# Written-out orders of work on every engine, and narrower warm-up matmuls in a PSUM bank of their own, in a four-layer linear-attention and SwiGLU kernel

## The chip, the core and the metric

The kernel runs on one core of a Trainium2 chip. The metric is the device time of one execution in microseconds, as the median of five runs. The engines have short names here: PE is TensorE (PEld its weight loads, which overlap its matmuls), DVE is VectorE, ACT is ScalarE, POOL is GpSimd, and SP is SyncE, which only issues DMAs.

## The reference

Two kinds of layer alternate, A, B, A, B (layers 0 to 3 below), on 2048 tokens of width 512; the weights of both A layers are the same, and so are those of both B layers. Everything is bf16.

```
x = A_x
x = x + A(layernorm(x), wqkv, wo)        # layer 0
x = x + B(layernorm(x), gate, up, down)  # layer 1
x = x + A(layernorm(x), wqkv, wo)        # layer 2
x = x + B(layernorm(x), gate, up, down)  # layer 3

A: q, k, v = x @ wqkv, in 32 heads of 16
   phi(t) = where(t > 0, t + 1, exp(t)) + 1e-6
   kv = sum_s phi(k)^T v ;  z = sum_s phi(k)
   o  = phi(q) kv / (phi(q) z + 1e-6) ;  A = o @ wo
B: silu(x @ gate) * (x @ up) @ down      # inner width 1792
```

## The kernel before

The tokens are cut into 16 tiles of 128, and four tiles make a group. All weights and the residual `X` stay in SBUF. PSUM has eight banks of 128x512 f32, `PB[0]` to `PB[7]`. The work of PE is written as a list of tokens, `PROGRAM`, and the recording functions below turn each token into operations on all engines. A token names the layer, the kind of step and the tile or group:

- `S` is a spin: a matmul of zeros that keeps PE busy at the start and that nobody reads.
- `0t1` transposes the normalized tile 1 of layer 0 on PE, and ACT or DVE copies it out. Only tiles named in `PE_T` go this way. All others are transposed by a DMA that SP issues (`xT`).
- `0k4` is the key projection of tile 4, four matmuls of 512 columns. Behind it ACT takes `exp`; DVE clips it (`ts`) and takes the maximum with `1 + k` (`phi`). For tiles named in `ON_ACT` ACT also makes `1 + k` (`id1`), so that DVE's `phi` does not read PSUM.
- `0g4` adds tile 4 to the matrix x^T phi(k), in four banks that are held from the first to the last tile of the layer. `0z4` adds it to the sum of phi(k), in one more held bank.
- `0q12` is the query projection of group 1, part 2, with the same `phi`; `0d12` its denominator. `den` on DVE ends in a reciprocal. In most groups ACT then repeats 1/den (`rep`), a DMA transposes it (`rT`) and DVE multiplies (`pqn`). In groups of `PE_T` (`0d2`, `2d1`) the tokens `0r20` to `0r23` do the same on PE.
- `0v` and `0m0` to `0m3` fold the value and output weights into the matrix; each `m` is copied out of PSUM (`evac`).
- `0w3` is the attention output of tile 3. `res` on DVE adds it to `X`.
- `1u012` is one gate/up pair of a B layer for group 0, inner block 12: eight matmuls into two banks. ACT takes `tanh`, DVE does `gst` (times gate) and `h` (times up). `1n3` is the down projection of tile 3, fourteen matmuls, and its `res`.

Behind each `w` and `n` the next layernorm is recorded by `ln`: ACT takes the sum of squares (`sq`), POOL a scaled sum (`negm`), POOL or DVE `vpe`, POOL the power -1/2 (`pow`), and then DVE applies mean and scale (`apply`), or, for tiles named `0x5` and the like in `ON_ACT`, POOL makes one more product (`nmr`) and ACT applies it. In layer 0 the statistics of `X` come from DVE, or from ACT for tiles named `0s4` and the like. Below, `1x6.apply` is that step of the layernorm that feeds tile 6 of layer 1.

Buffers bind the steps. Layernorms of layers 1 and 3 go through three buffers `xnB` in turn, and ACT's `sq` writes its unused output there, so the `sq` of a tile waits until the DMA transpose of the tile three earlier has landed. The gate/up pairs share three buffers `tht` between `tanh` and `h`. A step that needs a bank takes the free one that was used longest ago.

`Prog.op` records an operation with its buffers read and written, its assumed duration and a kind. `Prog.schedule` keeps PE in the order of `PROGRAM` and chooses the order of every other engine while the program is built: it simulates the engines, and among the operations that could start within `HOLD` it takes the one with the earliest due time, shifted by a `BIAS` of its kind. `Prog.sync` then reduces the dependences to semaphore waits, and `emit` writes each engine's list. On the chip every engine works through its list strictly in order.

The large weights come by POOL's queue. `Wo`, the four pieces `Wg0` to `Wg3` and the four pieces of `Wu` are loaded behind the last DMA transpose of layer 0, `Wd` in four pieces behind the first four transposes of layer 1.

## Time and profile before

| | |
|---|---|
| median of 5 runs | 432.77 us (432.57 to 433.63) |
| profiled execution, its own time | 431.64 us |
| its span (first to last instruction) | 429.9 us |
| granted clock of PE in the span | 1.0 |
| busy: PE, DVE, ACT, POOL | 419.4, 290.5, 214.8, 79.9 us |
| one matmul of 512 columns in a stream | 379 ns from start to end, the next starts about 216 ns after it |

A matmul's row shows its whole way through the array; in a stream the next one starts long before it ends. So PE's idle time in the rows is the time without any matmul under way, and a gap in the stream is longer than that by about 0.16 us (379 less 216 ns).

### The profile page before, as it was taken

To read this page: it belongs to the slowest core of one execution; us is meant where nothing else is said; L and a number is where in the kernel's file an instruction comes from. 1 tells how busy PE (TensorE), PEld (TensorE's weight loads), DVE (VectorE), ACT (ScalarE), POOL (GpSimd) and SP (SyncE) were. 2 spreads that over 40 slices of the span, in tenths; PEclk is the share of its full clock that TensorE was granted. 3 is DMA by queue.
4 is the path that set the end of the run, shared out by engine and by line. 5 is a ranking of instruction groups with operands and counts; after the bars stand their busy time and mean duration, and the time that the engine had idled before them with its cause. 6 is when DMAs were issued, how large, how long until landed. Compare 5 with 4: busy or idle time off the path is not lost.

```text
span 429.9 us, 6498 instructions
## 1 busy us (share of the span) xinstructions
PE 419.4 (98%) x2188; PEld 194.9 (45%) x2231; DVE 290.5 (68%) x593; ACT 214.8 (50%) x402; POOL 79.9 (19%) x231
## 2 busy tenths in 40 slices
PE   7999999999999999999999999999999999999997
PEld 3444544444444444444444454444444444444444
DVE  6966998695687448776454549989836727845762
ACT  5997785685445444254456736584422403412320
POOL 5842046213210220000213100621010100000000
PEclk9999999999999999999999999999999999999999
DMA  8659234541110020000111104262020110001001
GB/s 281 144 89 358 49 75 137 109 87 38 37 38 1 12 26 12 0 2 2 26 24 27 24 16 84 50 89 48 12 50 13 26 37 14 12 18 33 1 2 50
DMA packets 52738, 23.11 MB, mean 54 GB/s; under 512 B 45856, under 2 KB 51616, under 8 KB 52704
## 3 DMA queue, kind: packets, MB, share of 16 engines
q1 hardware_dynamic: 50864, 16.13, 18.4%
q0 software_dynamic: 1296, 6.03, 3.9%
q10 hardware_dynamic: 544, 0.52, 0.4%
q8 instruction: 18, 0.29, 0.3%
q14 instruction: 16, 0.13, 0.1%
HBM read 9.70 MB, written 2.10 MB: 27 GB/s over the span
## 4 chain that ended last, share of the span: by engine, by line
PE 89%; ACT 4%; issue 2%; POOL 2%; DMA 1%; DVE 1%; SPq 0%; ACTq 0%; DVEq 0%
PE pb L395 89%; ACT etmp L558 1%; POOL rstd L502 1%; ACT xnA L509 1%; DMA X<-in_A_x_dram 1%; ACT pq L561 1%; DMA xnT<-xnB 1%; DVE stats L478 0%; POOL vpe L498 0%; ACT xnB L509 0%; POOL nmr L506 0%; ACT pk L561 0%; ACT tht L773 0%; ACT xnB L489 0%; DVE pq L742 0%
## 5 line engine op out<-in xcount | busy, mean ns | idle before, releaser
L773 ACT ACTIVATE tht<-pb 128x512 f32<-128x512 f32 x112 | 66.1, 593 | 115.1 <-PE pb L395 112.8
L395 PE MATMUL pb<-xnT,Wg 128*128 128x512 bf16 x440 | 113.9, 379 | 1.1 <-DMA xnT<-xnB 0.6
L395 PE MATMUL pb<-xnT,Wu 128*128 128x512 bf16 x440 | 114.1, 379 | 0.7 <-DVE tht L775 0.2
L775 DVE SCALAR_TENSOR_TENSOR tht<-tht,pb 128x512 f32<-128x512 f32 x112 | 76.8, 685 | 34.8 <-ACT tht L773 30.6
L395 PE MATMUL pb<-Wd,hT 128*128 128x512 bf16 (+1 forms) x452 | 99.0, 373 | 0.5
L778 DVE TENSOR_TENSOR hT<-tht,pb 128x512 bf16<-128x512 f32 x112 | 77.0, 688 | 11.6
L395 PEld LDWEIGHTS pb<-Wd,hT 128*128 128x128 bf16 x462 | 45.2, 98 | 51.8 <-DVE hT L778 0.5
L395 PEld LDWEIGHTS pb<-xnT,Wu 128*128 128x128 bf16 x448 | 43.7, 98 | 53.6 <-ACT tht L773 0.7
L395 PEld LDWEIGHTS pb<-xnT,Wg 128*128 128x128 bf16 x448 | 43.4, 98 | 52.8 <-issue 1.3
L492 POOL TENSOR_SCALAR mv<-sums 128x1 f32<-128x1 f32 x50 | 11.9, 241 | 200.7 <-DVE X L753 113.1
L558 ACT ACTIVATE etmp<-pb 128x512 bf16<-128x512 f32 x64 | 37.2, 595 | 14.7 <-PE pb L395 12.2
L502 POOL TENSOR_TENSOR rstd<-vpe,negh 128x1 f32<-128x1 f32 x64 | 36.5, 571 | 30.6 <-DVE vpe L498 26.6
L563 DVE TENSOR_SCALAR etmp<-etmp 128x512 bf16<-128x512 bf16 x64 | 18.6, 291 | 23.2 <-ACT etmp L558 22.5
L801 DVE SCALAR_TENSOR_TENSOR pq<-pb,X 128x512 bf16<-128x512 f32 (+1 forms) x17 | 11.2, 660 | 32.6 <-PE pb L395 32.6
L395 PE MATMUL pb<-Wqkv,xnT 128*128 128x512 bf16 x124 | 31.2, 379 | 1.0 <-ACT xnT L544 0.4
L395 PE MATMUL pb<-xnT,Wqkv 128*128 128x512 bf16 x125 | 31.9, 378 | 0.2
L395 PE MATMUL pb<-GT,pq 128*128 128x512 bf16 x124 | 30.0, 379 | 1.6 <-DVE pq L742 0.9
L395 PE MATMUL pb<-pk,xnA 128*128 128x512 bf16 x122 | 30.1, 379 | 0.4
L489 ACT ACTIVATE xnB<-X,sums 128x512 bf16<-128x512 bf16 x32 | 22.9, 715 | 14.8 <-DMA xnT<-xnB 8.0
L801 DVE SCALAR_TENSOR_TENSOR X<-pb,X 128x512 bf16<-128x512 f32 x16 | 11.1, 692 | 18.8 <-PE pb L395 18.7
L509 ACT ACTIVATE xnA<-X,nmr,rstd 128x512 bf16<-128x512 bf16 x23 | 18.6, 811 | 10.0 <-POOL nmr L506 9.7
L753 DVE SCALAR_TENSOR_TENSOR X<-pb,X 128x512 bf16<-128x512 f32 x32 | 21.5, 685 | 0.8 <-PE pb L395 0.7
(70 smaller groups left out, 308.2 us busy)
## 6 DMA issues: line engine op xcount, KB each, us to landing
out_dram<-pq SPq DMA_DIRECT2D x15, 128.0 KB, 1.7
Wg<-in_B_w_gate_dram POOLq DMA_DIRECT2D x4, 448.0 KB, 5.0
Wu<-in_B_w_up_dram POOLq DMA_DIRECT2D x4, 448.0 KB, 4.8
X<-in_A_x_dram SPq DMA_DIRECT2D x6, 256.0 KB, 4.7
Wd<-in_B_w_down_dram POOLq DMA_DIRECT2D x3, 512.0 KB, 4.7
Wqkv<-in_A_wqkv_dram SPq DMA_DIRECT2D x2, 512.0 KB, 7.1
Wqkv<-in_A_wqkv_dram ACTq DMA_DIRECT2D x2, 256.0 KB, 3.3
X<-in_A_x_dram SPq DMA_DIRECT2D x4, 128.0 KB, 3.4
```

Of the source, the lines that this page charges most:

```text
L395: return op("pe", lambda e: e.matmul(o_ap, lhsT=lhsT, rhs=rhs, start=start, stop=stop, skip_group_check=skip), r=r, w=w, occ=occ, lat=occ ...
L489: op("act", lambda a: a.activation(out=b_ap, in_=X[:, t, :], func=ACT.Square, scale=-float(D), bias=sums[:, t:t + 1], accum_out=mv[:, t, 1 ...
L492: op("pool", lambda p: p.tensor_scalar(out=mv[:, t, 0:1], in0=sums[:, t:t + 1], scalar1=-1.0 / D, scalar2=None, op0=ALU.mult), r=[f"sm{t}" ...
L502: op("pool", lambda p: p.tensor_tensor(out=rstd[:, t:t + 1], in0=vpe[:, t:t + 1], in1=negh[:], op=ALU.pow), r=[f"vp{t}", "negh"], w=[f"rs{ ...
L509: op("act", lambda a: a.activation(out=b_ap, in_=X[:, t, :], func=ACT.Identity, bias=nmr[:, t:t + 1], scale=rstd[:, t:t + 1]), r=[xk, f"nm ...
L558: op("act", lambda a: a.activation(out=etmp[e][:], in_=PB[pb][:], func=ACT.Exp), r=[f"pb{pb}"], w=[f"e{e}"], occ=0.48, lat=0.55, kind="exp")
L563: op("dve", lambda v: v.tensor_scalar(out=etmp[e][:], in0=etmp[e][:], scalar1=1.0, scalar2=1e-6, op0=ALU.min, op1=ALU.add), r=[f"e{e}"], w ...
L753: op("dve", lambda v: v.scalar_tensor_tensor(out=X[:, t, :], in0=PB[pb][:], scalar=1.0, in1=X[:, t, :], op0=ALU.mult, op1=ALU.add, accum_o ...
L773: op("act", lambda e: e.activation(out=tht[a][:], in_=PB[pg][:], func=ACT.Tanh, scale=0.5), r=[f"pb{pg}"], w=[f"th{a}"], occ=0.48, lat=0.5 ...
L775: op("dve", lambda v: v.scalar_tensor_tensor(out=tht[a][:], in0=tht[a][:], scalar=1.0, in1=PB[pg][:], op0=ALU.add, op1=ALU.mult), r=[f"pb{ ...
L778: op("dve", lambda v: v.tensor_tensor(out=hT[h][:, j, :], in0=tht[a][:], in1=PB[pu][:], op=ALU.mult), r=[f"pb{pu}", f"th{a}"], w=[f"h{h}_{ ...
L801: op("dve", lambda v, pb=pb, lo=lo, hi=hi: v.scalar_tensor_tensor(out=o_ap[:, lo:hi], in0=PB[pb][:, 0:hi - lo], scalar=0.5, in1=X[:, t, lo ...
```

## The change

`Prog.schedule` no longer chooses. A table `ORDER` gives every operation's place on ACT, DVE, POOL and SP by its name, and `PROGRAM` gives PE's, as it did. The durations, the due times, `BIAS` and some unused code (`colsum`, `is_raw`) go. Both versions emit static lists; what differs is the order in them and the engine of some steps.

- Spins: 13 of 512 columns become 61 of 128 columns. They took a bank each in turn; now one bank is held for all of them until the first `q`.
- PE: 38 spins, `0t0`, 8 spins, `0k0`, `0t1`, 12 spins, `0t2`, 1 spin, `0k1`, `0t3`, 2 spins, `0k2`, `0k3`, `0g0`, and so on; it was 9 spins, `0t0`, 4 spins, `0t3`, `0t1`, `0k0`, `0t2`, `0k1`, `0k2`, `0g0`, `0k3`. `0t15` leaves PE, so SP issues one more DMA transpose. In layers 0 and 2 some `z`, `g`, `d`, `r` and `w` tokens trade places.
- Engines: 24 of 44 `apply` steps move from ACT to DVE, and their `nmr` on POOL goes. Four more tiles of layer 0 take their statistics on ACT (`0s1`, `0s6`, `0s10`, `0s13`, `0s15` in, `0s8` out). Seven more `id1` run on ACT, so seven `phi` on DVE no longer read PSUM. One more `evac` moves from DVE to ACT (`2G3`), five more `vpe` from POOL to DVE.

```diff
 PROGRAM = """
-S S S S S S S S S 0t0 S S S S 0t3 0t1 0k0 0t2 0k1 0k2 0g0 0k3 0z0 0g1 0k4 0g2 0g3 0k5 0z4 0k10 0z2 0k9 0g4 0g5
-0k6 0z10 0k7 0z9 0z3 0q03 0k8 0g10 0t15 0g7 0k15 0k13 0z5 0z8 0k12 0g9 0k11 0q11 0g6 0z15 0k14 ...
+S ... (38) 0t0 S S S S S S S S 0k0 0t1 S ... (12) 0t2 S 0k1 0t3 S S 0k2 0k3 0g0 0g1 0k4 0g2 0g3 0k5 0k10 0g4 0k9 0g5 0z0
+0k6 0k7 0g10 0q03 0z4 0z2 0k8 0z10 0k15 0z9 0g7 0k13 0g9 0k12 0k11 0z3 0q11 0z5 0z8 0g6 0k14 ...
...
-2d22 2q30 ... 2r10 2v 2q33 2m1 2m0 2m2 2m3 2w0 2d31 2r11 2d30 2w1 2r13 2w2 2w3 2r12 2w6 2w5 ...
+2q30 2d22 ... 2r10 2v 2q33 2m0 2m1 2m2 2d31 2m3 2w0 2r11 2d30 2w1 2d32 2r13 2w2 2r12 2w3 2w6 2w5 ...
...
-0q31 0m0 0m1 0m3 0m2 0r21 0r23 0w3 0r22 0w2 0w1 0r20 0w0 0q33 0w5 0w11 0w7 0w6 0w9 0q32 0d33 0w8 0w4 0w10 1u011
+0q31 0m1 0m0 0m3 0m2 0r21 0r23 0w3 0r20 0w2 0w1 0r22 0q33 0w0 0w5 0w11 0q32 0w7 0w6 0w9 0d33 0w8 0w4 0w10 1u011
 """
+ORDER = {
+    "act": """
+i.ld i.ld1 i.c 0x1.stats 0x1.sq 0t0.xT 0x4.stats 0x4.sq 0t1.xT 0k0.exp 0t2.xT 0x10.stats 0k1.exp 0x10.sq 0k2.exp
+...
+1u002.tanh 1x6.sq 1u006.tanh 1u012.tanh 1x9.sq 1u003.tanh 1x4.sq 1u013.tanh
+...
+2q32.exp 2d2.rep1 2d2.rep2 2q33.exp 2M0.evac 2M2.evac 2q33.id1 2d2.rep3 3x0.sq ...
+""",
+    "dve": """
+i.c 0x0.stats 0x0.aggr 0x0.vpe 0x0.apply 0x2.stats 0x3.stats 0x2.aggr 0x3.aggr 0x1.apply 0x5.stats 0x2.apply
+0x9.stats 0x3.apply 0x8.stats 0x5.aggr 0x4.apply 0t3.xT 0k0.ts 0k1.ts 0k0.phi 0k1.phi 0x5.apply 0k2.ts 0x8.aggr
+...
+0q33.phi 1x0.apply 0w5.res 0w7.res 0w6.res 0q32.ts 1x5.vpe 0w9.res 0w10.res 0w8.res 1u011.gst 0w4.res 1u011.h
+1x5.apply 1u007.gst 1u007.h 0q31.ts 0q31.phi 1u005.gst 1u008.gst 1u005.h 1x7.vpe 1u002.gst 0q32.phi 1u008.h 1u002.h
+1x7.apply 1x6.apply 1u006.gst 0q30.ts 1u012.gst 1x9.vpe 0q30.phi 1u006.h 1u012.h 1u003.gst 1x9.apply 0d3.den
+0d3.den1 1x4.apply 1u003.h 1u010.gst 1u013.gst 1u013.h 1u010.h ...
+... 2M1.evac 2M3.evac 2d0.pqn3 2w0.res 2r11.pqn 2w1.res 2r13.pqn 3x0.apply 2r12.pqn 2w2.res ...
+... 3n14.res 3n13.res 3n12.res 3n15.res 3n15.res1
+""",
+    "pool": """
+i.c i.c3 i.c4 0x0.pow 0x1.negm 0x1.vpe 0x1.pow 0x2.vpe 0x2.pow 0x3.vpe 0x3.pow 0x4.vpe 0x4.pow 0x4.negm i.c1 i.c2
+... i.ld8 i.ld7 i.c5 i.c6 i.ld5 i.ld3 i.ld6 i.ld i.ld2 i.c7 1x3.negm i.ld4 ... 1x1.pow 1x0.negm i.ld1 1x0.pow
+1x5.pow 1x11.vpe 1x11.pow 1x5.negm 1x11.negm 1x11.nmr 1x7.pow 1x6.negm 1x6.vpe 1x8.negm 1x7.negm 1x9.negm
+1x6.pow 1x4.negm Wd.ld Wd.ld3 1x9.pow Wd.ld1 Wd.ld2 1x10.negm 1x4.vpe 1x4.pow 1x10.pow ...
+""",
+    "sp": """ ... 0x4.xT 0x5.xT 0x10.xT 0x9.xT 0x6.xT 0x7.xT 0x8.xT 0x15.xT 0x13.xT 0x12.xT 0x11.xT 0x14.xT ... """,
+}
 PE_T = set("""
-0t0 0t1 0t2 0t3 0d2 0t15 2d1
+0d2 0t0 0t1 0t2 0t3 2d1
 """.split())
...
     def schedule(self):
-        ... (the simulated list scheduling)
+        self.order = {"pe": [o for o in self.ops if o.eng == "pe"]}
+        for e in self.ENGINES[1:]:
+            by = {o.name: o for o in self.ops if o.eng == e}
+            self.order[e] = [by.pop(x) for x in ORDER[e].split()]
+            assert not by, f"without a place on {e}: {list(by)}"
...
+        warm = bank(pin=True)
+
         def spin():
-            warm = bank()
-            mm(warm, zero[:, 0:P], zero, True, True, r=[f"h1_{NF - 1}"], w=[f"pb{warm}"], occ=0.427)
+            mm(warm, zero[:, 0:P], zero[:, 0:P], True, True, r=[f"h1_{NF - 1}"], w=[f"pb{warm}"], n=P, cols=(0, P))
...
+            if tok[1] == "q" and not pq_of:
+                pinned.discard(warm)
```

In `ORDER`, `i.ld` of POOL is `Wo`, `i.ld1` is `Wg0`, `i.ld2` `Wu0` and so on to `i.ld8`, `Wu3`; `Wd.ld` to `Wd.ld3` are the four pieces of `Wd`.

## The prediction

> **What bounds the kernel now.** I read the page first, for the engine that bounds the span.

> ```profile
> span 429.9 us, 6498 instructions
> PE 419.4 (98%) x2188; PEld 194.9 (45%) x2231; DVE 290.5 (68%) x593; ACT 214.8 (50%) x402; POOL 79.9 (19%) x231
> ```

> PE is busy for all but 10.5 us, and its matmuls hardly change (four transposes go), so the change can only win where PE stands still. The windows view, cut by stage, says where; its columns are the stretch and its length, busy us of PE, PEld, DVE, ACT and POOL, PE's clock, DMA share and GB/s.

> ```profile
> 0.00:8.69 8.69, 6.29 (x24) 2.43 (x25) 5.48 (x16) 3.66 (x6) 3.85 (x17) 1.00 0.80 262
> 8.69:26.00 17.31, 16.39 (x102) 7.63 (x102) 14.90 (x45) 16.94 (x32) 12.55 (x34) 1.00 0.69 152
> 80.00:91.00 11.00, 10.02 (x48) 4.19 (x48) 9.08 (x17) 10.16 (x22) 3.64 (x10) 1.00 0.25 48
> 91.00:237.00 146.00, 145.32 (x665) 66.17 (x677) 93.22 (x183) 72.15 (x136) 23.26 (x72) 1.00 0.12 22
> 237.00:272.00 35.00, 33.36 (x277) 16.92 (x282) 23.75 (x54) 22.59 (x43) 4.14 (x14) 1.00 0.21 42
> ```

> In 91 to 237 us PE has no hole to fill. In the first 26 us ACT is nearly full (16.94 of 17.31 us), and in 80 to 91 us again (10.16 of 11), with DVE at 9.08. PE's timeline shows the holes one by one (start, length, operation; in brackets PE's idle time and what ended it). A hole in the stream is 0.16 us longer than the idle time, for a matmul's end (379 ns) overlaps the next start (216 ns).

> ```profile
> 5.92 1.49 PE L395 MATMUL pb<-hT 128*128 128x512 bf16 x4
> 8.75 1.03 PE L395 MATMUL pb<-Wqkv,xnT 128*128 128x512 bf16 x4
> 11.27 1.04 PE L395 MATMUL pb<-Wqkv,xnT 128*128 128x512 bf16 x4 [0.40 <-ACT xnT L544]
> 25.35 1.02 PE L395 MATMUL pb<-Wqkv,xnT 128*128 128x512 bf16 x4 [0.36 <-ACT etmp L558]
> 90.84 1.02 PE L395 MATMUL pb<-xnT,Wg 128*128 128x512 bf16 x4 [0.64 <-DMA xnT<-xnB]
> 265.71 1.02 PE L395 MATMUL pb<-GT,pq 128*128 128x512 bf16 x4 [0.41 <-ACT GT L649]
> 271.54 5.35 PE L395 MATMUL pb<-GT,pq 128*128 128x512 bf16 x24 [0.85 <-DVE pq L742]
> ```

> The holes: the head until the first projection at 8.75; 0.52 us at 25.35; about 0.35 at the first `0w` (55.53); three in 81 to 91, of 0.24, 0.37 and 0.80, together 1.4; 0.57 at 265.71 and 1.01 at 271.54. Less than 4 us beside the head.

> **The work that moves.** ACT loses 24 applies of 0.81 and gains four statistics of 1.70, seven `id1` of 0.69 and one evacuation of 0.59: -7.3 us. DVE gains 24 applies of 0.41 (9.8) and five `vpe` (0.7), loses four statistics of 0.85, an evacuation, a copy, and 0.27 on seven `phi`: +4.1. POOL loses 6.7. None of it is on the path by itself: DVE goes from 290 to 295 of 430 us. It counts where an engine is full.

> **Head, +1.1 (0.3 to 1.7).** DVE applies tile 0 as soon as `pow` ends at 4.63; before, another tile's statistics stood ahead until 5.00. The 512-column spins start 0.427 us apart, so 38 of a quarter fill 1.24 to 5.31. Then: `0t0` 5.31, ACT's copy 5.95 to 6.55, `0k0` at 6.6 (was 8.75). Tile 1 has its statistics on ACT (4.40 to 5.95), then `vpe`, `pow`, `apply` to 7.35; `0t1` behind `0k0` at 7.7, its copy behind ACT's `0x4.sq` at 8.15 to 8.75; `0k1` at 8.9 (9.83). `0k0.exp` waits behind that copy, to 9.2, without harm: its reader on DVE stands behind `0t3.xT` and behind `0k1.ts`, which waits for `0k1.exp`, which waits behind `0x10.stats` to 10.9. So `0k0.phi` ends at 11.85, just as `0k3` does; `0g0` and `0g1` run to 13.6. The next token, `0k4`, needs the first DMA transpose. It is issued at 10.4 (was 11.10). Before, it took 3.30 us and landed at 14.41, just behind the last of `Wqkv` at 13.84; so now 13.7 to 14.4. `0k10` then starts at 17.2 to 17.9, where before the same work led to 18.19: +0.3 to +1.0. Behind it, the hole at 25.35 (ACT late) should go with ACT's applies, +0.5, and `0t15` takes 0.22 off PE. I take 1.1, near the late landing, the row that this transfer resembles most. SP's twelfth transpose (1.19 us of issue) moves the nine weight loads behind it by 2 us; they were done by 43.5 and are first needed at 54. `Wg0` is now loaded behind `1x0.negm`, near 62, lands in 5.0 us (the row of `Wg`), and `1u011` needs it near 68: covered by 1 us, and 1 to 2 us if that cover goes. The held bank leaves two banks for `0k6` and `0k7`; by ACT's order both are read out 0.5 us early.

> [...]

> **The first `0w`, +0.1 (0 to 0.3).** `0m1` comes first, so DVE starts its evacuation 0.2 us earlier.

> **81 to 91 us, +0.7 (-2.2 to 1.4).** Before, `1x5.pow` stood on POOL behind three `Wd` loads (69.36 to 72.67), its transpose was issued at 74.61 into that traffic and landed after 4.9 us, and `sq` of tiles 6, 8, 9 and 4 followed late, in front of `tanh`s. Now `1x5.pow` and `1x6.pow` go first, the applies are on DVE, and tile 5 is issued near 72, into a quiet queue. But the loads now wait behind `1x6.vpe`, which waits for `1u002.tanh` and `1x6.sq` near 78: behind it stand four loads, `1x9.pow` and `1x4.vpe`. The loads took 8.8 us in all, so 79 to 87, and the transposes of tiles 6, 7, 9 and 4 (80 to 86) fall into them. The view of the transposes shows the price of that: here for the three issued among the loads, then for all.

> ```profile
> DMA to landing us min/median/max: 4.1/4.7/4.9
> DMA to landing us min/median/max: 2.4/2.4/4.9
> ```

> Tile 6 then lands at 84.5 instead of 82.3, `1x4.sq` holds up the `tanh`s behind it, and `1x4.apply` on DVE ends near 87, with `1u003.h` and four more behind it. Two banks that PE wants near 88 come 0.2 to 0.7 late; tile 4 lands at 89.7 to 92 and `1u110` wants it at 89.5. I take 0.7 us of holes in place of 1.4; the worst, 2.6 and 1.0, is 3.6.

> [...]

> **265 to 272 us, +1.0 (0.3 to 1.2).** The 1.01 at 271.54 was `2w6` waiting for DVE's product behind `2r12`, directly ahead of it. Now `2r12` stands before `2w3`, whose four matmuls (0.86) cover the product (0.68): +0.85 to 1.0. `2M0.evac` goes ahead of `2q33.id1` (0.1), and `2d31` fills 0.1 of its wait. What comes next: `3x3` must land for `3u008` near 277.2, 7.0 us after `2w3`; by its chain (`res` to 272.1, `sq`, `pow` to 274.0, `apply`, 2.4 to land) 276.9. If late, up to 0.7 goes back.

> **Elsewhere, 0.** 91 to 237 and 290 to 417 us run at PE's pace, with DVE at 64%. At the end DVE takes `3n14` before `3n13` and `3n12`: 2.1 us within the last tile's 3.0; 0.2 lost if it does not fit.

> **Sum:** 1.1 + 0.1 + 0.7 + 1.0 = 2.9 us. The profiled execution took 431.64 (span 429.9 and 1.7 around it), so 428.7 there, span 427.0; against the median of 432.77, 429.9. All low ends: -1.6, so 434.4; all high ends: +4.6, so 428.2.

> **The rivals.**
> - *The late `Wd` loads cost a new hole.* Place: `1u110`. It decides if tile 4's transpose is still issued among the loads, that is, if they end after about 86. For it: the 4.7 us landings. Against it: ACT and DVE no longer wait for `nmr`. Hole of 3.6 and low ends elsewhere: 434.4.
> - *Only the order around `2r12` pays.* The transposes land where they did, and holes elsewhere are refilled by DVE, which is as full as ACT was: 0.3 + 0 + 0 + 0.8 = 1.1, so 431.7. [...]
> - *All the holes go:* 428.2.

> **How the numbers follow.** About 0.2%, 0.87 us, is what a measurement can tell, so faster is under 431.9 and slower over 433.6. Chances: forecast 0.56 (its own range 428.9 to 431.2), the rivals 0.17, 0.19 and 0.08. Faster: 0.56, 0.08 and 0.11 of the second rival, 0.75; same: the other 0.08; slower 0.17. The range 427.9 to 433.8 leaves out most of the slower case.

> **What would show it.** Right: `0k0` near 6.6, `0k4` near 14, no hole above 0.2 us before `0k8` (25 before) and before `2w6` (271 before), and the hole before `1u110` below 0.6. Wrong: `0k4` after 14.8; holes over 1 us between 80 and 92, ended by a DMA `xnT<-xnB` or DVE `hT`; new holes inside the B layers.

## The result, and the profile after

The changed kernel takes 436.04 us (median of 28 runs, 433.21 to 440.14), the kernel before 432.69 us beside it (47 runs, 431.64 to 434.81): ratio 1.0069, 95% interval 1.0057 to 1.0082. It is slower by 3 us where 2.9 less was forecast, and outside the range of 427.9 to 433.8. Its runs also spread over 7 us, those of before over 3. The profiled execution is its fastest, 433.21 us, so this profile shows only part of the loss; a second profile of the unedited kernel stands beside it below.

First the top of the page after. PE is busy for 0.9 us more than before, and the span is 1.5 longer. Some matmuls have no row in the profiles (by the count of PEld 43 before and 44 after), so small differences of PE's busy time should not be read closely.

```profile
span 431.4 us, 6378 instructions
PE 420.3 (97%) x2231; PEld 197.5 (46%) x2275; DVE 282.0 (65%) x612; ACT 206.0 (48%) x402; POOL 72.0 (17%) x206
```

The windows view of after, with the columns of the prediction (last: PE's clock, DMA share, GB/s):

```profile
26.00:56.00 30.00, 28.88 (x230) 14.20 (x232) 21.20 (x55) 24.01 (x45) 5.26 (x10) 1.00 0.59 150
56.00:70.00 14.00, 13.56 (x68) 5.66 (x69) 12.14 (x36) 9.10 (x21) 6.60 (x16) 1.00 0.59 122
80.00:91.00 11.00, 10.14 (x54) 4.43 (x53) 8.89 (x19) 4.30 (x10) 5.41 (x10) 1.00 0.82 215
237.00:272.00 35.00, 34.50 (x285) 17.70 (x290) 23.12 (x56) 21.59 (x42) 3.95 (x11) 1.00 0.19 38
```

and of before in the two stretches that the prediction left out:

```profile
26.00:56.00 30.00, 29.56 (x233) 14.95 (x236) 22.90 (x57) 24.75 (x46) 5.28 (x9) 1.00 0.56 174
56.00:70.00 14.00, 13.95 (x73) 6.29 (x74) 13.66 (x39) 9.85 (x22) 7.24 (x22) 1.00 0.29 58
```

Read 80 to 91 us first: ACT fell from 10.16 us of work to 4.30, yet PE is busy for 10.14 of 11 as it was for 10.02, and DMA carries 215 GB/s in place of 48. The full engine was emptied and nothing came of it. In 26 to 56 and 56 to 70 us, where before had next to no holes, PE idles 0.7 and 0.4 us more, and in the latter DMA's share rose from 0.29 to 0.59. In 237 to 272 us PE is busy for 1.1 us more (34.50, was 33.36): the hole in front of 2w6 is filled.

One figure of the page misleads. DVE's busy time fell from 290.5 to 282.0 us, though its work grew: the times of its single instructions sum to 3.7 us more than before, near the 4.1 that the prediction has. Busy time counts overlapping instructions once, and in the new order neighbours on DVE overlap more.

PE's timeline names the holes. Of the profiled run after:

```profile
14.23 1.04 PE L407 MATMUL pb<-Wqkv,xnT 128*128 128x512 bf16 x4 [0.84 <-DMA xnT<-xnA]
41.60 1.02 PE L407 MATMUL pb<-xnT,Wqkv 128*128 128x512 bf16 x4 [0.38 <-DVE pq L574]
52.58 0.90 PE L407 MATMUL pb<-GT,Wqkv 128*128 128x128 bf16 x13 [0.26 <-ACT GT L624]
67.67 1.90 PE L407 MATMUL pb<-GT,pq 128*128 128x512 bf16 x8 [0.27 <-DVE X L725]
89.63 1.04 PE L407 MATMUL pb<-xnT,Wg 128*128 128x512 bf16 x4 [0.53 <-DVE hT L750]
279.51 1.02 PE L407 MATMUL pb<-xnT,Wg 128*128 128x512 bf16 x4 [0.53 <-DMA xnT<-xnB]
```

and of the second profile, with a span of 435.2 us:

```profile
70.86 1.02 PE L407 MATMUL pb<-xnT,Wg 128*128 128x512 bf16 x4 [1.40 <-DMA xnT<-xnB]
90.87 1.04 PE L407 MATMUL pb<-xnT,Wg 128*128 128x512 bf16 x4 [0.55 <-DVE hT L750]
93.75 1.02 PE L407 MATMUL pb<-xnT,Wg 128*128 128x512 bf16 x4 [0.58 <-DVE hT L750]
100.84 2.33 PE L407 MATMUL pb<-Wd,hT 128*128 128x512 bf16 x9 [1.54 <-DVE hT L750]
```

The holes of before at 25, 55 and 271 us are gone, as the change meant. New ones stand at 41, 52, 67 to 71, 90 to 101 and 279 us, and those between 67 and 101 differ from run to run.

Starts of PE's steps in the traces, minus the same step's in before, give the ledger (last column: end of the last matmul). The experiments' rows are explained below.

| profiled run | 0k14 | 0w2 | 1u011 | 1u106 | 2v | 3u008 | end |
|---|---|---|---|---|---|---|---|
| before, us | 34.53 | 56.61 | 68.41 | 103.78 | 262.42 | 278.66 | 427.35 |
| after | -1.32 | +0.38 | +1.23 | +1.12 | +1.12 | +0.85 | +0.85 |
| after, second | -1.24 | +0.51 | +2.46 | +4.62 | +4.62 | +4.16 | +4.55 |
| `down_moved` | -1.39 | +0.36 | +0.89 | -0.28 | -0.27 | -0.53 | -0.06 |
| `loads_moved` | -0.95 | +0.50 | +0.47 | -0.93 | -0.93 | -1.03 | -0.66 |
| `before_late_down` | +0.22 | +0.20 | +0.20 | +4.40 | +4.39 | +4.36 | +4.36 |
| `before_r12` | +0.62 | +0.61 | +0.60 | +0.05 | +0.05 | -0.59 | -0.58 |

The profiled run: the head wins 1.32; 34 to 57 us give 1.70 back; 57 to 68 lose 0.85; 68 to 104 win 0.11; 262 to 279 win 0.27; 0.7 is lost behind the last matmul. Sum +1.5. The second run has the same head and loses 1.95 in 57 to 68 and 2.16 in 68 to 104.

### The profile page after: what moved, and what is told of

Its sections match the earlier page's. It is cut to its first block, busy times and chain, and to the rows that moved or that the text cites. A ratio compares the mean times of both kernels' runs of the same rounds, so it can differ in the third digit from the quotient of the medians.

```text
span 431.4 us, 6378 instructions
## 1 busy us (share of the span) xinstructions
PE 420.3 (97%) x2231; PEld 197.5 (46%) x2275; DVE 282.0 (65%) x612; ACT 206.0 (48%) x402; POOL 72.0 (17%) x206
## 4 chain that ended last, share of the span: by engine, by line
PE 85%; DMA 6%; DVE 3%; ACT 3%; issue 2%; POOL 1%; SPq 0%; DVEq 0%; ACTq 0%
PE pb L407 85%; DMA xnT<-xnB 3%; DMA RT<-rrep 2%; DMA X<-in_A_x_dram 1%; DMA xnT<-xnA 1%; DVE X L725 1%; POOL rstd L509 1%; ACT etmp L562 1%; ACT GT L624 0%; DVE hT L750 0%; DVE tht L747 0%; DVE xnB L520 0%; SPq L438 0%; ACT pq L565 0%; ACT xnB L496 0%
## 5 line engine op out<-in xcount | busy, mean ns | idle before, releaser
L745 ACT ACTIVATE tht<-pb 128x512 f32<-128x512 f32 x112 | 64.7, 595 | 134.1 <-PE pb L407 111.1
L747 DVE SCALAR_TENSOR_TENSOR tht<-tht,pb 128x512 f32<-128x512 f32 x112 | 75.2, 684 | 42.7 <-ACT tht L745 40.6
L750 DVE TENSOR_TENSOR hT<-tht,pb 128x512 bf16<-128x512 f32 x112 | 73.8, 683 | 2.8
L505 POOL TENSOR_SCALAR vpe<-mv 128x1 f32<-128x1 f32 x43 | 9.0, 209 | 98.9 <-ACT xnB L496 78.9
L496 ACT ACTIVATE xnA<-X,sums 128x512 bf16<-128x512 bf16 x22 | 15.9, 722 | 20.2 <-DVE X L773 20.1
L773 DVE SCALAR_TENSOR_TENSOR X<-pb,X 128x512 bf16<-128x512 f32 x16 | 11.1, 691 | 21.8 <-PE pb L407 21.8
```

The lines of the kernel that those rows point to most:

```text
L496: op("act", lambda a: a.activation(out=b_ap, in_=X[:, t, :], func=ACT.Square, scale=-float(D), bias=sums[:, t:t + 1], accum_out=mv[:, t, 1 ...
L505: op(vp_on, lambda p: p.tensor_scalar(out=vpe[:, t:t + 1], in0=var, scalar1=scale, scalar2=1e-5, op0=ALU.mult, op1=ALU.add), r=[vk], w=[f" ...
L745: op("act", lambda e: e.activation(out=tht[a][:], in_=PB[pg][:], func=ACT.Tanh, scale=0.5), r=[f"pb{pg}"], w=[f"th{a}"], kind="tanh")
L747: op("dve", lambda v: v.scalar_tensor_tensor(out=tht[a][:], in0=tht[a][:], scalar=1.0, in1=PB[pg][:], op0=ALU.add, op1=ALU.mult), r=[f"pb{ ...
L750: op("dve", lambda v: v.tensor_tensor(out=hT[h][:, j, :], in0=tht[a][:], in1=PB[pu][:], op=ALU.mult), r=[f"pb{pu}", f"th{a}"], w=[f"h{h}_{ ...
L773: op("dve", lambda v, pb=pb, lo=lo, hi=hi: v.scalar_tensor_tensor(out=o_ap[:, lo:hi], in0=PB[pb][:, 0:hi - lo], scalar=0.5, in1=X[:, t, lo ...
```

## The experiments

All ran 5 rounds beside the kernel before. Ratios are to before on the same chip, with 95% intervals. Theories are named by letters in the expectations: A, a wait in DVE's list makes tile 0 late; B, the narrow spins make the clock uncertain; C, SP's transposes land late because weight loads of POOL's queue are under way; D, the harm of C is done by instructions that wait for such a landing at the head of ACT's or DVE's list; E, DVE is too full with the applies; L, the harm of C is done by the late landing itself.

**The changed kernel again** (`after_again`, no edit).

> The changed kernel, unedited, for a second profile: its runs spread from 433.2 to 440.1 us about a median of 436.0, while the profiled one was the fastest of all. Theory A (a wait at the head of DVE's queue and transposes caught among weight loads): the same places lose again, 1u011 about 1.2 us later than before and 3u008 about 0.9, and what a slower run loses more is lost at a wait on a DMA of tile 0, 6, 9 or 4 between 60 and 92 us. Theory B (the clock): a slower run loses its time before 20 us, with TensorE's full rate granted later than 4.4 us or granted and taken back, and a mean clock below 1.0. Median near 436 by both.

434.95 us, 1.0051 (1.0031 to 1.0070). Second profile: shown above. Its holes of 1.40 us at 70.86, ended by a DMA `xnT<-xnB`, and of 1.54 us at 100.84, ended by `hT`, are new holes inside a B layer, which the prediction named as a sign of being wrong; the two ended by `hT` near 91 and 94 us are under the 1 us that it named for 80 to 92. The extra loss is at 1u011 and between 85 and 104 us; at 0k4 the two profiles agree to 0.1 us (14.23 and 14.31). So C with A or D; not B.

**DVE's sums ahead of the waiting products** (`w0_first`).

```diff
-0r20.pqn 0r22.pqn 0d1.pqn3 0d1.pqn2 0w0.res 0w11.res 1x1.apply 0d1.pqn
+0r20.pqn 0r22.pqn 0w0.res 0d1.pqn3 1x1.apply 0d1.pqn2 0w11.res 0d1.pqn
```

> The changed kernel with two DVE instructions moved: 0w0.res ahead of 0d1.pqn3, 1x1.apply ahead of 0d1.pqn2; nothing else. In the changed kernel these stood behind the two products, which wait for DMA transposes of q's denominators (landed 61.85 and 62.98), so 0w0.res ran at 63.35 where its bank was ready near 61. Theory A: 0w0.res near 61.4, tile 0's transpose issued 1.3 to 1.9 us earlier, 1u011 back to within 0.3 us of before (68.4 to 68.7, it was 69.64), and 0.9 to 1.3 us less in all: median 434.7 to 435.1. Theory C (tile 0's transpose lands late because of Wg's load beside it, not because it is issued late): 1u011 gains less than 0.4 us, median within 0.4 of 436. Theory B: no change in the median.

434.58 us, 1.0039 (1.0019 to 1.0060): 0.4 below the unedited kernel on that chip, where the two intervals overlap. The hole before 0w4 went and tile 0's transpose was issued 0.8 us earlier than in the second profile (66.17, was 66.97), but landed at 70.08, so PE still waited for it for 1.04 us at 1u011. A is a small part at most.

**All late loads earlier** (`loads_early`).

```diff
-i.ld i.ld2 i.c7 1x3.negm i.ld4 1x3.vpe ... 1x0.negm i.ld1 1x0.pow 1x5.pow 1x11.vpe ... 1x11.nmr 1x7.pow
+i.ld i.ld2 i.ld1 i.ld4 i.c7 1x3.negm 1x3.vpe ... 1x0.negm 1x0.pow 1x5.pow 1x11.vpe ... 1x11.nmr Wd.ld Wd.ld3 Wd.ld1 Wd.ld2 1x7.pow
```

> The changed kernel with POOL's order alone changed: the loads Wg0 and Wu1 go behind Wu0, with the other weight loads (near 40 us), and the four Wd loads go from behind 1x6.vpe (80.7 to 85.1 us) to directly behind 1x11.nmr (near 71.4). Theory C (transposes caught among weight loads make the loss and the spread): tile 1's transpose takes 2.4 us in place of 3.7, 1u011 gains 0.3 to 0.5; tiles 6, 7 and 9 land in 2.4 to 3 us in place of 4.4 to 5.8; 1u110 waits less by 0.4; the spread of runs narrows to about 2 us, and the median falls by 1 to 2.5, to 433.5 to 435. Theory A (tile 0 is late by DVE's order): 1u011 gains at most 0.5, median 435.3 to 435.8, spread unchanged. Theory B: no change in median or spread.

434.43 us, 1.0034 (1.0014 to 1.0054). The place was ill chosen, and tells much. Tiles 1 and 0 now landed in 2.4 us, and 1u011 waited for nothing. But `i.c7`, which builds the mask, came behind two loads, and PE stood 1.3 us at 42 us for it; and tile 5's transpose, issued at 74.32 right behind four `Wd` loads, landed at 82.47 after 8.15 us, 0.45 behind the last load (82.02). ACT's `1x6.sq` waited for its buffer until 82.50, and holes of 1.05 and 0.73 us at 85 and 87 us followed.

**Before with the narrow spins** (`before_narrow_spins`).

```diff
-S S S S S S S S S 0t0 S S S S 0t3 0t1
+S x38 0t0 S x16 0t3 0t1
```

> The kernel before, its orders written out as lists, with the changed kernel's spins alone: 128 columns, in a bank that is held, 38 ahead of 0t0 and 16 behind it in place of 9 and 4 of 512 columns. Theory B (narrow spins make the clock uncertain): the runs spread like those of the changed kernel, over 4 us, and the median is 1 to 3 us above before's. Theories A and C: median within 0.4 us of before, lowest to highest within 2.5 us; TensorE's full rate comes between 4.3 and 5.5 us, where it came at 6.8.

433.44 us, 1.0018 (0.9997 to 1.0038): no difference that the interval shows. So the loss of 1 to 3 us that B expected did not come, and spins by themselves bring nothing either. The runs spread over 4.6 us (432.11 to 436.70), which is B's sign and not that of A and C, and in the profile PE's full rate came at 6.70 us, not between 4.3 and 5.5. Two runs make the spread: their mean granted clock was 0.996 and 0.992, and the other ten, at 1.0, lie within 2.5 us. Before has such runs too (six of 35 on that chip at 0.996). B falls as the cause of the loss; that narrow spins add to the spread is not shown.

**No weight load between 55 and 100 us** (`no_down_loads`; the `Wd` products see zeros).

```diff
-                dma("pool", Wd[:, c:c1, :], ..., w=[f"Wd{j}" for j in range(c, c1)], after=after)
+                op("pool", lambda g, c=c, c1=c1: g.memset(Wd[:, c:c1, :], 0.0), w=[f"Wd{j}" for j in range(c, c1)], kind="ld")
-i.ld2 i.c7 1x3.negm ...
+i.ld2 i.c7 i.ld4 i.ld1 Wd.ld Wd.ld3 Wd.ld1 Wd.ld2 1x3.negm ...
```

> The changed kernel without the four loads of Wd (POOL writes zeros there near 41 us instead, so the last product of each B layer is left out of the result) and with Wg0 and Wu1 loaded directly behind i.c7, near 41 us: between 55 and 100 us no weight load is under way. Everything else as changed. Theory C (SP's transposes land only when the weight loads issued shortly before them have landed, and ACT's sq and DVE's apply wait for that at the head of their queues): every transpose of tiles 0 to 9 lands 2.4 to 2.6 us after its issue; 1u011 within 0.3 us of before's 68.4 (plus 0.4 from stalls ahead of 55 us); no hole over 0.3 us before 1n3; 1u106 at or ahead of before's 103.8; median 432.0 to 433.3 and a spread under 3 us. Theory E (DVE's longer list in 81 to 101 us, with 24 more applies, is itself too slow): holes of 0.5 to 1.5 us ended by hT on DVE stay near 89 and 99, 1u106 1 us or more behind before, median 434 to 435.

437.21 us, 1.0105 (1.0087 to 1.0122), for a reason of its own: POOL's four writes of zeros ran from 42.77 for 6.2 us, and a DVE step beside them, of a form that took 0.28 us at 41.98, ended 0.16 us behind them, with PE behind it for 5.2 us:

```profile
43.44 5.69 DVE L574 TENSOR_SCALAR etmp<-etmp 128x512 bf16<-128x512 bf16 x1
```

Behind that stall it answers the question. From 62 to 270 us PE's timeline has no hole at all; 1u011 to 1u106 takes 33.96 us where before takes 35.37 and the two profiles of after take 35.26 and 37.53. The applies on DVE do not hold PE up: E falls. C stands.

**Five places mended** (`waits_moved`): the edit of `w0_first`, the loads as in `loads_moved` below, and

```diff
-0d1.rep1 0G0.evac 0G2.evac 0G3.evac      (ACT)
+0G0.evac 0G2.evac 0G3.evac 0d1.rep1
-0q00.ts 0q01.ts 0q00.phi 0q01.phi        (DVE)
+0q00.ts 0q00.phi 0q01.ts 0q01.phi
+                    at = {o.lane: k for k, o in enumerate(mine) if o.dma}
-                    for q, v in sorted(self.final.items()):
+                    for q, v in sorted(self.final.items(), key=lambda x: at.get(x[0], -1)):
```

> The changed kernel with its lists mended at five places, all its work kept: 0d1.rep1 behind the three G evacuations on ACT; 0q00.phi ahead of 0q01.ts, 0w0.res ahead of 0d1.pqn3 and 1x1.apply ahead of 0d1.pqn2 on DVE; Wu1 and Wg0 loaded behind i.c7; the four Wd loads near where before had them (behind 1x0.pow, 1x5.pow and 1x11.nmr); at the end SP waits last for the lane of the last store. Theory C: 0v 0.6 to 0.8 us earlier against the changed kernel, 1u011 at 67.8 to 68.5, tile 5 lands near 79.5 after 5 us but tiles 6, 9 and 4 in 2.4 to 3; holes of 81 to 101 us together under 1.5 (before: 1.4); the end 0.3 to 0.6 us shorter behind the last landing; median 431.5 to 433.2. Theory E: 1u011 the same gain, but 1 to 2 us of holes by hT on DVE stay behind 85 us: 433.3 to 434.5.

431.72 us, 0.9974 (0.9959 to 0.9990): faster than before. The loads alone bring as much (`loads_moved`, below), so no gain of the four other places is shown.

**The late `Wd` loads put into the kernel before** (`before_late_down`).

```diff
-1x4.negm Wd.ld 1x7.vpe 1x7.pow Wd.ld1 Wd.ld2 1x5.pow 1x5.nmr Wd.ld3 1x10.negm 1x11.pow 1x11.nmr 1x6.pow 1x6.nmr
+1x4.negm 1x7.vpe 1x7.pow 1x5.pow 1x5.nmr 1x10.negm 1x11.pow 1x11.nmr 1x6.pow Wd.ld Wd.ld1 Wd.ld2 Wd.ld3 1x6.nmr
```

> The kernel before, its orders written out as lists, with one edit: the four Wd loads behind 1x6.pow (near 81 us) in place of 69 to 74. That is the place which the changed kernel gives them, under before's other orders (applies of tiles 6, 9 and 4 on ACT). Theory C: transposes of tiles 6, 8, 9 and 4 land 4 to 6 us after issue, ACT's 1x4.sq and 1x10.sq wait for them with tanh behind, 1u106 1.5 to 4 us later than before, median 434 to 436.5. Theory E: the loads cost before's order under 0.5 us, since DVE has fewer applies: 432.7 to 433.2.

435.72 us, 1.0058 (1.0038 to 1.0077). This one edit takes before to where the changed kernel is. Tile 6, issued at 82.57, landed at 88.22, 0.47 behind the last load. PE's timeline shows two holes; from 93.29, in the second of them, PE's clock was halved for 3.4 us (0.87 over 91 to 104 us), which cost another 1.4:

```profile
91.17 1.02 PE L413 MATMUL pb<-xnT,Wu 128*128 128x512 bf16 x4 [1.83 <-DVE tht L753]
93.83 1.86 PE L413 MATMUL pb<-xnT,Wg 128*128 128x512 bf16 x4 [1.64 <-DVE tht L753]
```

```profile
91.00:104.00 13.00, 11.19 (x45) 4.67 (x46) 11.27 (x21) 7.94 (x16) 1.80 (x6) 0.87 0.37 73
```

The mean granted clock of each run separates the two parts: the four runs at 1.0 took 433.56 to 434.10 us, the two at 0.996 (as in this profile) 435.48 and 435.95, the four at 0.992 436.35 to 436.61. At full clock the loss is thus about 1.4 us (434.0 against 432.59, the median of before's runs at 1.0); the rest of the 3.0 comes in the runs whose clock dropped.

**`2r12` alone** (`before_r12`).

```diff
-2r13 2w2 2w3 2r12 2w6                 (PE)
+2r13 2w2 2r12 2w3 2w6
-3x0.apply 2w2.res 2r12.pqn 2w3.res    (DVE)
+3x0.apply 2r12.pqn 2w2.res 2w3.res
```

> The kernel before, its orders written out as lists, with 2r12 ahead of 2w3 on TensorE and its product ahead of 2w2's sum on DVE, as the changed kernel has them. By the prediction's term 2w6 comes 0.85 to 1.0 us earlier and 3u008 0.3 to 1.0 earlier: median 431.8 to 432.4. By the changed kernel's profile the gain stops at 3u008, which waits for tile 3's transpose whatever comes earlier: 2w6 0.9 to 1.3 us earlier, 3u008 at most 0.3 us earlier, median 432.5 to 432.8.

431.68 us, 0.9974 (0.9958 to 0.9991). 2w6 came 0.94 us earlier against 2v, as predicted; 3u008 then waited 0.17 us for tile 3 (a hole of 0.31 with the overlap), and 0.64 was left.

**Own buffers for the normalized tiles** (`own_buffers`).

```diff
-                b = r_xb.take(1)
-                b_ap, bk = xnB[b][:], f"xb{b}"
+                b = None
+                b_ap, bk = xnA[:, t, :], f"xa{t}"
...
-            if L % 2 and f"{L}t{t}" not in PE_T:
-                r_xb.done(b)
```

> The changed kernel with one edit: in the B layers the normalized tile t goes to its own slot of xnA (unused there) in place of a ring of three xnB buffers, so no sq and no apply waits for the landing of an earlier tile's transpose. Lists and loads as changed; the transposes themselves still land late among the weight loads. If the damage is done by waits at the head of ACT's and DVE's queues (theory D): 1x6.sq, 1x4.sq and 1x10.sq start as their statistics' inputs are there, tanh and h behind them are not held, holes ended by hT between 81 and 101 us fall below 0.4 in all, 3u008 0.3 to 0.6 earlier, 1u011 unchanged; median 434.0 to 434.8, spread smaller by half. If the late landing itself is what counts (theory L: PE waits for tiles 0 and 4): holes ended by a DMA take their place at 1u011 and 1u110, 1 to 2 us, median 435 to 436.

434.57 us, 1.0046 (1.0025 to 1.0066); the unedited kernel had 1.0051 on another chip. ACT's and DVE's waits for the ring were gone: in the waits view of 60 to 102 us the unedited kernel's second profile has

```profile
ACT xnB L496 <- DMA xnT<-xnB: 6.0, 3, 3.1
DVE pq L699 <- DMA RT<-rrep: 2.4, 3, 1.4
PE pb L407 <- DMA xnT<-xnB: 1.4, 1, 1.4
```

and here the first is absent. In this profile nothing was won by it: tile 4 was issued at 89.12, 1.2 us earlier, behind a fourth `Wd` load that landed at 95.14, and itself landed at 96.03; 1u110 started at 96.27 behind 3.63 us of idle PE, and a stretch at a lower clock followed (windows view, PE's clock third from the end):

```profile
92.00:96.00 4.00, 0.64 (x3) 0.10 (x1) 2.69 (x6) 2.48 (x5) 1.55 (x4) 1.00 0.98 97
96.00:100.00 4.00, 3.73 (x10) 1.43 (x11) 0.42 (x1) 0.00 (x0) 0.00 (x0) 0.57 0.16 32
```

So L for this execution: it waited for the landing itself, and D only decides at which step that shows. But the profiled execution is the slowest of the ten (439.11 of 432.65 to 439.11 us), and the median lies in D's range, not in L's; the intervals of the two kernels overlap. That own buffers bring nothing to the changed kernel is not shown beyond that.

**The loads alone** (`loads_moved`): POOL's order as before had it, nearly, all else as changed.

```diff
-i.ld2 i.c7 1x3.negm i.ld4 ... 1x0.negm i.ld1 1x0.pow 1x5.pow 1x11.vpe ... 1x11.nmr 1x7.pow
+i.ld2 i.c7 i.ld4 i.ld1 1x3.negm ... 1x0.negm 1x0.pow Wd.ld 1x5.pow Wd.ld3 1x11.vpe ... 1x11.nmr Wd.ld1 Wd.ld2 1x7.pow
-1x6.pow 1x4.negm Wd.ld Wd.ld3 1x9.pow Wd.ld1 Wd.ld2 1x10.negm
+1x6.pow 1x4.negm 1x9.pow 1x10.negm
```

> The changed kernel with POOL's order alone changed, as in the version with five mended places: Wu1 and Wg0 behind i.c7 near 41 us, the four Wd loads behind 1x0.pow, 1x5.pow and 1x11.nmr near 69 to 75 us. Theories D and L both: transposes of tiles 2, 1 and 0 land in 2.4 us, 1u011 0.5 to 0.8 us earlier than in the changed kernel (tile 0 is still issued late by DVE's order), tiles 6, 9 and 4 in 2.4 to 3 us; holes from 81 to 101 us under 1.2; median 433.0 to 434.2: two thirds or more of what the five mends together brought (4.3 of the changed kernel's 436.0, to 431.7). If the lists' waits on ACT and DVE ahead of 70 us made most of it: 434.5 to 435.5.

431.36 us (431.02 to 433.56), 0.9975 (0.9960 to 0.9990): better than expected, as much as the five mended places brought, and a spread of 2.5 us. The view of the transposes in 78 to 93 us, of after's second profile and of this one:

```profile
DMA to landing us min/median/max: 3.3/4.9/6.6
```

```profile
DMA to landing us min/median/max: 2.4/2.4/2.5
```

and PE's windows over the same stretches, after's second profile and this one:

```profile
80.00:91.00 11.00, 10.38 (x55) 4.71 (x55) 8.90 (x20) 4.56 (x12) 6.34 (x14) 1.00 0.73 194
91.00:104.00 13.00, 10.59 (x47) 4.36 (x47) 9.08 (x17) 7.01 (x14) 1.55 (x4) 1.00 0.48 55
```

```profile
80.00:91.00 11.00, 11.00 (x57) 5.01 (x55) 10.56 (x23) 6.84 (x16) 3.50 (x11) 1.00 0.28 55
91.00:104.00 13.00, 13.00 (x62) 5.90 (x61) 8.66 (x19) 4.00 (x7) 0.68 (x2) 1.00 0.29 57
```

**Which loads** (`down_moved`: the four `Wd` loads of `loads_moved` alone; `gate_moved`: `i.ld4` and `i.ld1` alone).

> The changed kernel with the four Wd loads alone moved, from behind 1x6.vpe (80.7 to 85.1 us) to behind 1x0.pow, 1x5.pow and 1x11.nmr (near 70 to 76); Wg0 and Wu1 stay late, at 58 and 64 us. If the transposes of tiles 6, 9 and 4 among the Wd loads make most of the loss (the prediction's slower rival): 1u011 still 1 to 2.5 us behind before, but no hole over 0.8 between 85 and 101; median 432.2 to 433.5. If Wg0 and Wu1 in front of tiles 2 to 0 make most of it: 434 to 435.5.

> The changed kernel with Wu1 and Wg0 alone moved, behind i.c7 near 41 us; the Wd loads stay behind 1x6.vpe. If Wd makes most of the loss: tiles 2, 1 and 0 land in 2.4 us and 1u011 is 0.3 to 0.8 behind before, yet holes of 1.5 to 4 us stay between 85 and 101; median 434 to 435.3. If Wg0 and Wu1 make most of it: 432.2 to 433.5.

433.15 us, 0.9998 (0.9980 to 1.0017), and 434.26 us, 1.0028 (1.0003 to 1.0053). Against the changed kernel's 1.0069, `Wd`'s place is worth 0.7% and that of `Wu1` and `Wg0` 0.4%: 3.1 and 1.8 us. Both together brought 0.94%. These runs were on different chips. Against the 1.0051 of `after_again` the 0.5% of `Wd` and the 0.8% of both still stand clear of the intervals, but the 0.2% of `Wu1` and `Wg0` does not. For those the trace speaks: in `gate_moved` 57 to 68 us lose 0.06 us, where the two profiles of after lose 0.85 and 1.95.

**Mended places and own buffers** (`waits_own`: the edits of `waits_moved` and `own_buffers`), **then Wq and Wv behind the first transposes** (`waits_own_wq`).

```diff
-i.ld9 i.ld10 i.ld11 0x4.xT 0x5.xT 0x10.xT 0x9.xT ... 0x14.xT 0d0.rT      (SP)
+i.ld9 0x4.xT 0x5.xT 0x10.xT i.ld10 0x9.xT ... 0x14.xT i.ld11 0d0.rT
```

> The version with five mended places, and own slots of xnA for the normalized tiles of the B layers. Theory D: tile 5's late landing (near 79.7) no longer holds 1x6.sq, and 3x3.sq no longer waits for tile 0's landing: 81 to 92 us without a hole over 0.3, 3u008 0.4 to 0.7 earlier against 2w10; median 430.6 to 431.4. Theory L: as the five mends alone, 431.5 to 432.0.

> The version with five mended places and own slots, with SP's order changed once more: the loads of Wq (first needed at 23.8 us) behind 0x10.xT and of Wv (first needed near 52) behind 0x14.xT; in the changed kernel both stand ahead of 0x4.xT. If the first transpose lands with the input loads ahead of it, 0x4 lands near 13 in every run, 0k4 starts at 13.1 to 13.5 without a hole over 0.3, and the runs draw together: median 429.3 to 430.3, lowest to highest under 3 us (before: 429.9 to 436.7). If not, a hole of 1 to 2.5 us stays before 0k4 in some runs, median 431.0 to 431.8; and 0x9's transpose, now behind Wq, may come late for 0k9: up to 1 us back.

431.47 us, 0.9980 (0.9959 to 1.0001), and 432.44 us, 0.9989 (0.9971 to 1.0007): neither beats the loads alone. In the first, PE stood 2.3 us for a late `0x4`, and the clock was halved behind it (last section). In the second, `0x4` landed at 13.57 and the hole before 0k4 went, but `0x9`, now behind the load of Wq, came late, and two holes stood there, of 0.36 us at 18.09 and this one:

```profile
21.67 1.02 PE L414 MATMUL pb<-Wqkv,xnT 128*128 128x512 bf16 x4 [1.69 <-DMA xnT<-xnA]
```

**The version that beats both** (`before_r12_own`: before, with `2r12` moved and own buffers; `before_r12_own_wq`: Wq and Wv moved too).

> The kernel before as lists with 2r12 moved ahead of 2w3, and own slots of xnA for the normalized tiles of the B layers. The holes of before at 81 to 91 us (1.4 together) shrink to 0.5 to 0.9 and the 0.3 ahead of 3u008 goes: median 430.4 to 431.2. Theory L: no change from 431.7.

> The kernel before as lists, with 2r12 ahead of 2w3, own slots of xnA in the B layers, and Wq behind 0x10.xT and Wv behind 0x14.xT on SP. Before's 0k4 starts at 14.83 without a hole, for its chain is later than the landing; so the move should bring nothing by itself here: median 429.8 to 430.4, as without it (430.14). If 0k4 was waiting for the landing in most runs: 429.2 to 429.8.

430.14 us, 0.9940 (0.9924 to 0.9956), and 430.21 us, 0.9931 (0.9909 to 0.9954). Before's three holes in 81 to 91 us are gone; the gain is more than expected:

```profile
80.00:91.00 11.00, 11.00 (x58) 4.99 (x55) 9.37 (x17) 9.76 (x20) 3.34 (x10) 1.00 0.38 74
```

ACT is nearly as full here as it was in before (9.76 of 11 us, was 10.16). Own buffers pay here though tiles 5, 7 and 11 still land late (4.9, 4.0 and 3.0 us); tiles 6, 8, 9 and 4 land in 2.4. In the changed kernel, where tiles 6, 7 and 9 take up to 6.6 us, no gain shows.

## Why the prediction was wrong

**81 to 91 us, the step that failed.** The forecast was +0.7, its low end and the slower rival -2.2. The rival's mechanism is what happened: `before_late_down` reproduces it alone (+3.0 us of median, 1.4 in the runs at full clock), and `down_moved` takes it away (3.1 us). Its place was wider than `1u110`: the profiled run after has its hole at `1u000` (89.63), the second at `1u000`, `1u110` and `1n3`. The rival gave 434.4 and a chance of 0.17. What decided, in its own words, was whether the loads end after about 86. The text put them at 79 to 87 and still chose the good side. They were issued from 80.66, for POOL reached them late, and the last landed at 90.63 in the profiled run and 92.69 in the second: 10.0 and 10.8 us for the four, where before took 8.8. `1x9.pow` stands among them, and the transposes of tiles 6, 7 and 9 were issued beside them (81.25 to 85.28 in the profiled run); which of these made them longer was not tested. The view of the four loads in the profiled run after (first and last issue, then issue to landing):

```profile
L438 POOL DMA_DIRECT2D Wd<-in_B_w_down_dram x4: 716/768/836, 80.7 to 84.3; - x4
DMA to landing us min/median/max: 4.1/5.3/6.3
```

The price was too low as well: the prediction took 4.7 us for a landing, from three transposes at the edge of the loads. Those in the midst took 5.4, 4.4 and 5.8 us, in the second run 5.4, 4.4 and 6.6.

**`Wg0` behind `1x0.negm`, the second.** "Covered by 1 us, and 1 to 2 us if that cover goes" looked at the load's own landing, and that was in time (68.22). What it cost was the transposes beside it: tile 1 took 3.7 us, in the second run 5.2, and tile 0 stands behind it. `Wu1`, issued at 57.77, did the same to two transposes of 1/den (`0d1.rT3` and `rT2`: 4.75 and 4.6 us, 2.4 before), whose products stand ahead of `0w0.res` on DVE. 57 to 68 us lost 0.85 and 1.95; `gate_moved`, which moves both loads, takes this loss away. The prediction priced the transposes beside the `Wd` loads (4.7 us a landing) and not those beside these two.

**"Elsewhere, 0", the third.** 1.70 us went between 34 and 57 us, where before had only the 0.35 us at the first `0w`. There the written lists put a wait on a landing ahead of work that PE needs: ACT's `0d1.rep1` needs a buffer that a transpose held until 50.37, and the evacuations of `GT` for `0v` stood behind it (0.81 lost from 0v to 0m3; 0.31 in `waits_moved`, which moves it). 0.69 went between 0q12 and 0q13, 0.51 of it as a hole, for `0q00.phi` frees 0q13's bank late; the other order of these steps in `waits_moved` did not change that (0.60). In the stretch from 290 us, which was to run at PE's pace, seven of the traces with the changed head have one more hole, near 346 us inside `3n4` and ended by DVE's `hT`, that costs 0.36 to 0.47 us; the profile after has none.

**The tail.** The order `3n14`, `3n13`, `3n12` on DVE cost nothing, as predicted. But from the end of the last matmul to the end of the span 3.25 us pass, 2.56 in before: at the end SP waits for every lane in the order of their names; with one more transpose on SP the last store fell on an early lane, and five more waits of 0.07 us followed its landing. Waiting for the last store's lane last brought it to 2.90 (`waits_moved`); the rest lies in SP's closing steps.

**265 to 272 us, right in mechanism, off in size.** 2w6's hole went: 1.0 of 1.0. Then the prediction's own condition came in: `3x3` was expected at 276.9 for a need at 277.2; it landed at 279.26 where PE was ready near 278.8, and 0.67 went back, as much as the text had named. The transpose itself took 2.94 us for the 2.4 that the text gave it. 0.27 was left, 0.64 where `2r12` is moved alone.

**Head, right in seven of eleven profiles.** 1.32 at 0k14 for 1.1 predicted, 0k0 by 6.66 for 6.6, 0k4 at 14.23 for 14; and finer spins bring nothing by themselves (`before_narrow_spins`, 1.0018). Of the eleven profiled runs with the changed head, seven win 0.95 to 1.39 us at 0k14. In the other four (`waits_moved`, `gate_moved`, `own_buffers`, `waits_own`) the first DMA transpose lands 2.3 us later, 0k4 stands past 16 us, where 14.8 was the prediction's sign of being wrong, and 0k14 comes 0.9 to 2.7 us later than in before. That the profile after shows the term whole is luck in part. When PE's full rate comes differs as well: at 6.84 us in before, 5.6 behind the first spin, at 4.40 in the profile after, 3.2 behind it, and at 6.70 in `before_narrow_spins`; what sets the moment is not shown.

With the loads put back the change gives 431.36, 0.25% below before. In that kernel's profiled run the head wins 0.95, 34 to 57 us lose 1.45, 68 to 104 win 1.40, for before's three holes are gone (the best case of that term in the prediction), 262 to 279 win 0.10, the hole in `3n4` takes 0.37 and the tail 0.69: this run (431.67) is no faster than before's (431.64), while the medians differ by 1.2. The rest of the loss is the place of six load instructions.

**The spread** has several parts, and the runs do not settle how large each is. The changed kernel spread over 6.9 us in 28 runs and over 3.9 in 12; with the loads put back (`loads_moved`) it was 2.5, but `waits_own`, without those collisions, spread over 6.7. One part shows in the mean granted clock of each run: four of the 28 had 0.996 and took 436.9 to 440.1 us; the other 24, at 0.999 or 1.0, took 433.2 to 438.2. Another is the first DMA transpose. In the 11 profiled runs with the changed head it landed at 14.1 to 14.6 in seven and at 16.4 to 16.7 in four, each time where the input loads had ended after 14.5 us, and 0k4 stood 2.5 us. Why those loads end some 0.8 us later in some runs was not found; the changed order is not needed for it, for in `before_narrow_spins` it landed at 16.46 too. Taking Wq and Wv from in front of it only moved the wait.

## What to carry to other kernels

When a change moves a load on POOL's queue, list the transposes that will be issued while it is under way, and price each at the landing of the last load in front of it, not at its usual time (here 5.4 us for tile 6 beside the `Wd` loads, usually 2.4): that the load itself is in time for its own reader says nothing. An engine that was full is not what the stage waits for until the transfers behind it have been checked. In a list written by hand, each instruction that waits for a DMA landing or for a buffer that a DMA reads should stand behind everything that PE needs sooner.

## What the runs showed of the hardware

```profile
16.00:20.00 4.00, 3.46 (x9) 1.27 (x10) 2.04 (x6) 1.49 (x4) 1.52 (x5) 0.57 0.52 99
```

- In `no_down_loads` one DVE step, usually 0.28 us, ran for 5.69 us, from 43.44 to 49.13, beside POOL's four memsets (42.77 to 48.97). What held it is not shown.
